# Batch 2's local score visits merged into one, a second buffer for transposed strided keys, and an undivided last sum

## The chip, the core and the metric

One core of a Trainium2 chip runs the kernel. The metric is the device time in microseconds (us) of one execution; the median of several executions stands for a kernel. A profile is one more execution, recorded by the hardware profiler.

## What is computed

Eight batches of eight-head attention over 576 positions with head size 64, then a two-layer network with squared relu:

```
scores = scale * q @ k^T                       # 8 batches, 8 heads, 576 x 576, scale 1/8
mask_local   = (rel >= 0) & (rel < 32)         # heads 0 to 3
mask_strided = (rel >= 0) & (pos % 32 equal)   # heads 4 to 7
attn = softmax(where(mask, scores, -1e9));  x = attn @ v      # -> x: 4608 x 512
out  = relu(x @ w_in) ** 2 @ w_out             # 512 -> 2048 -> 512
```

Inputs and output are fp32 in memory; the kernel computes in bf16, with fp32 sums.

## The kernel before

The network is cut into nine chunks of 512 tokens. `mm1` (L855) makes one of 16 hidden blocks: four matmuls of 128x512 into a PSUM bank (of two, "ph", in turn), a relu on ScalarE (L869), and a square on VectorE (L873), issued one step later. `mm2` (L958) is a quarter of one output block: four matmuls, after the fourth quarter a copy on ScalarE (L973) and a store through SP. The last two chunks use sums of weights and activations in seven products (`mm2_7`, L922).

The attention is woven into these groups. The main loop (L1175) counts groups n; before group n it runs the words of line n of `PLAN`. Chunk 0's mm1 are groups 0 to 15, its mm2 16 to 31, chunk 1's mm1 32 to 47, its mm2 48 to 63; chunk 2 begins at group 64, and reads tokens of batch 2. A function passed to `later(n, ...)` (L483) is issued at the end of the n-th group from there (with n = 1, the current one); `put_off` (L664) does that and also marks PSUM banks as unread, so that nobody takes them. Nothing reorders afterwards: each engine executes in the order of issue, and semaphores hold an instruction until its inputs and its buffer are ready.

Two heads make a unit; units 8 and 9 are batch 2's local heads, 10 and 11 its strided ones; 12 and 13 are batch 3's local ones. The words that matter here:

- `l`, `c`, `T`: load q or k of local units, cast to bf16 (`cast_qk_local`, L313, VectorE), and transpose on TensorE (`step_T`, L502) with a copy out of PSUM (L509). `T9kv`: unit 9's keys, copied by VectorE. `A12q`: the transpose of unit 12's queries by a DMA from SP (L403).
- `S8!` (`step_S`, L527): scores of unit 8, twelve matmuls of 128x96 (L554), alternately of the two heads in the two halves of TensorE's rows, into four PSUM banks. With "!", the four exponentials of 128x288 (L570) are issued at once, and the masks (L576, VectorE) one and two groups later. `S9!` is the same for unit 9.
- `G3` (`step_G`, L590): the scores of both local units of a batch in one visit of 24 matmuls (L599) into six banks, six exponentials of 128x384 (L610) at once, four mask products (L606). Row 0 and row 1 are the first and second heads of both units. Batches 3 to 7 use it; batch 2 uses S8 and S9. The exponentials lie in `es01`: 576 columns of unit 8, directly behind them 576 of unit 9, for each row.
- `D8.0`, `D8.1` (`step_D`, L814): exp times values for one head, six matmuls (L822), then a reciprocal (L827) and a product (L828) on VectorE. Each matmul reads 128 columns of the exponentials, from column 96 n on.
- `E8` (L837): the result is transposed into `xt` by a DMA from SP; mm1 reads `xt`.
- `H2v` (L460): a copy of batch 2's values on VectorE.
- `C4k`, `X4k` (L365, L370): load of a batch's strided q or k, and its transpose by a DMA from SP into a buffer of `strTs` (two for q, one for k). `s2` and `x2` (L679, L707): batch 2's strided scores, and its sums and output; `x2+2+5` puts the second and third part off by 2 and 5 groups. `k21v` (L386) copies a part of the strided keys.
- `Q`, `R`, `U`, `V`, `B`: other loads and copies of the following batches.

The last product of the last chunk ("3", L945) writes the right half of the last 128 rows in two sums of 128 columns (L948), each stored directly, the first by ScalarE's queue and the second by SP's (L949).

Of the kernel before, what the change touches and what calls it, by code (L numbers as in the profile page):

```python
# [10 lines left out]
AF = mybir.ActivationFunctionType  # L11
ALU = mybir.AluOpType
# [37 lines left out]
33: T8kv  # L50
34: C3q T8qv
35: T9qa
36: H2v
38: C3k S8!
39: c12kv A12k T9kv
40: c13kv A13k
41: D8.0
42: S9! D8.1
44: E8 c12qv A12q
45: k21v D9.0 c13qv A13q  # L60
46: D9.1
47: U3
48: s2 Q16k E9
50: Q17q Q16q
52: Q17k
54: x2+2+5
55: X3k X3q
56: C4k C4q
57: V3 R12kv
58: V4 R12qa  # L70
# [79 lines left out]
def kernel(  # L150
# [48 lines left out]
    v_st = rows.enter_context(tc.tile_pool(name="v_st", bufs=1, side="right"))  # L199

    PS = bass.MemoryType.PSUM
    strTs = {nm: rows.enter_context(tc.tile_pool(name=f"strT{nm}", bufs=n, side="right")) for nm, n in (("q", 2), ("k", 1))}
    psum = ctx.enter_context(tc.tile_pool(name="psum", bufs=1, space=PS))
    psb = psum.tile([128, 8, 512], FP32, name="psb")
    all_banks = [psb[:, i] for i in range(8)]
# [277 lines left out]
    def later(n, fn, key=None):  # L483
        pending.append((clock[0] + n, key, fn))
# [102 lines left out]
        later(3, lambda: expo(1, 1), u)  # L587
        later(4, lambda: masks(1), u)

    def step_G(b):  # L590

        us = (4 * b, 4 * b + 1)
        bk = [bank("pt") for _ in range(6)]
        bk = [bk[0::2], bk[1::2]]
        for t in range(2 * NL):
            for row in range(2):
                s, j = st[us[t // NL]], t % NL
                rows, c = slice(64 * row, 64 * row + 64), QL * (t % 4)
                nc.tensor.matmul(bk[row][t // 4][:, c:c + QL], s["kT"][rows, QL * j:QL * j + 128],  # L599
                                 s["qT"][rows, QL * j:QL * (j + 1)], start=True, stop=True)  # L600
        e = es01.rearrange("p (r c) -> p r c", r=2)

        def masks(row):
            x = e[:, row, 0:2 * S].rearrange("p (u t c) -> p u t c", u=2, c=QL)
            for i in range(2):
                nc.vector.tensor_tensor(x[:, i], x[:, i], mask_all, op=ALU.mult)  # L606

        for row in range(2):
            for i in range(3):
                nc.scalar.activation(e[:, row, 4 * QL * i:4 * QL * (i + 1)], bk[row][i][:, 0:4 * QL], AF.Exp, scale=scale)  # L610
            later(row + 2, lambda row=row: masks(row), ("G", b, row))

    def blocks(part):
        return range(NJ * part, min(NJ * (part + 1), NB))
# [199 lines left out]
    def step_D(u, part):  # L814
        run_due(lambda x: x[1] in (u, ("G", u // 4, part)))
        s = st[u]
        e = es01[:, 2 * ER * part + S * (u % 4):] if u > 11 else es[u % 4][:, ER * part:]
        rhs = s["v"].rearrange("p h t d -> p (h t) d")
        po = bank("pt")[:, 0:NL * (D + 1)].rearrange("p (n d) -> p n d", d=D + 1)
        for n in range(NL):  # L820
            c = QL * n
            nc.tensor.matmul(po[:, n, :], e[:, c:c + 128], rhs[:, NL * part + n, 0:D + 1], start=True, stop=True)  # L822
        if part == 0:
            s["x"] = xl_pool.tile([QL, 2 * NL, D], BF16, name="x_l")
        x = s["x"].rearrange("p (t h) d -> p h t d", h=2)[:, part]
        rinv = small.tile([128, NL, 1], FP32, name="rinv")
        nc.vector.reciprocal(rinv[0:QL], po[0:QL, :, D:D + 1])  # L827
        nc.vector.tensor_tensor(x, po[0:QL, :, 0:D], rinv[0:QL].to_broadcast([QL, NL, D]), op=ALU.mult)  # L828
# [93 lines left out]
    def mm2_7(c, i):  # L922
        n, u = ORDER7[i // 2], i % 2
        g, r0 = gs[c], 512 * c + 256 * u
        t0 = slice(256 * u, 256 * u + 128)
        if n == "1":
            ys[c, u] = [y_pool.tile([128, 512], FP32, name="y") for _ in range(2)]
            ys[c, u, "p"] = [bank("pt")]
        if n == "6":
            ys[c, u, "p"].append(bank("pt"))  # L930
        y1, y2 = ys[c, u]
        lo, hi = slice(0, 256), slice(256, 512)
        pa = ys[c, u, "p"][n not in "124"][:, lo]
        for k in range(8):
            a = g[:, k, t0] if n == "1" else g[:, 8 + k, t0] if n == "2" else \
                ss[{"6": "2", "7": "3", "4": "a", "5": "1", "3": "4"}[n]][:, k, u]
            b = w_out_b[:, k, lo] if n == "1" else w_out_b[:, 8 + k, lo] if n == "2" else \
                ts[{"6": "2", "7": "3", "4": "4", "5": "1", "3": "b"}[n]][:, k]
            nc.tensor.matmul(pa, a, b, start=k == 0 and n not in "273", stop=k == 7, skip_group_check=True)  # L939
        if n in "12":  # L940
            nc.scalar.copy((y2 if n == "1" else y1)[:, lo], pa)
            return
        to, by = {"6": (y1[:, hi], y2[:, lo]), "7": (y2[:, hi], y2[:, lo]), "4": (y2[:, lo], y2[:, hi]),
                  "5": (y2[:, hi], y2[:, hi]), "3": (y1[:, hi], y1[:, hi])}[n]
        if n == "3" and c == NCH - 1 and u:  # L945
            nc.sync.dma_start(out=out[r0:r0 + 128, lo], in_=y1[:, lo])
            for h, eng in ((0, nc.scalar), (128, nc.sync)):
                nc.vector.tensor_tensor(to[:, h:h + 128], pa[:, h:h + 128], by[:, h:h + 128], op=ALU.add)  # L948
                eng.dma_start(out=out[r0:r0 + 128, 256 + h:384 + h], in_=to[:, h:h + 128])  # L949
            return  # L950
        nc.vector.tensor_tensor(to, pa, by, op=ALU.add)  # L951
        if n in "53":
            r0 += 128 * (n == "5")
            nc.sync.dma_start(out=out[r0:r0 + 128, :], in_=y2 if n == "5" else y1)
# [40 lines left out]
    def run_step(word):  # L995
# [3 lines left out]
        if op == "w":  # L999
            warm(int(arg))  # L1000
        elif op == "c":
            cast_qk_local(int(arg[:-2]), arg[-2], ENG[arg[-1]])
        elif op == "T":
            step_T(int(arg[:-2]), arg[-2], ENG[arg[-1]])
        elif op == "W":
            step_TS(int(arg[0]), arg[1], int(arg[2]), ENG[arg[3]])
        elif op == "S":
            u, _, half = arg.rstrip("!").partition(".")
            step_S(int(u), int("!" in arg), [int(half)] if half else range(2))
        elif op == "G":  # L1010
            step_G(int(arg))
        elif op == "b":
            step_B(*(int(x) for x in arg.split(".")))
        elif op == "N":
            step_N(int(arg))
        elif op == "O":
            step_O(int(arg))
        elif op in "sx" and "." in arg:
            (step_SS if op == "s" else step_XX)(*(int(x) for x in arg.split(".")))
        elif op == "s":  # L1020
            step_S4(int(arg))
        elif op == "x":
            b, _, pace = arg.partition("+")
            step_X4(int(b), [0] + [int(x) for x in pace.split("+")])
        elif op == "k":
            step_K(int(arg[0]), int(arg[1]), ENG[arg[2]])
        elif op == "m":
            memset_later(arg[:-1], nc.gpsimd if arg[-1] == "g" else nc.vector)
        elif op == "D":
            if "." in arg:  # L1030
                u, part = arg.split(".")
                step_D(int(u), int(part))
            else:
                step_D0(int(arg))
        elif op == "E":
            step_E(int(arg.rstrip("av")), ENG.get(arg[-1]))
        elif op == "P":
            first_part(int(arg[0]), int(arg[1]))
        elif op == "H":
            shift_v_local(int(arg[:-1]), ENG[arg[-1]])  # L1040
        elif op == "C":
            load_str_tall(int(arg[:-1]), arg[-1])
        elif op == "Q":
            load_qk_rows(int(arg[:-1]), arg[-1])
        elif op == "X":
            transpose_str(int(arg[:-1]), arg[-1])
        elif op == "A":
            transpose_cast(int(arg[:-1]), arg[-1])
        elif op == "R":
            order_local(int(arg[:-2]), arg[-2], ENG[arg[-1]])  # L1050
        elif op == "Y":
            transpose_local(int(arg))
        elif op == "V":
            load_v_local_sw(int(arg))
        elif op == "U":
            load_v_str(int(arg))
        elif op == "B":
            spread_v_str(int(arg[0]), int(arg[1]), ENG[arg[2]])
        elif op == "l":
            load_qk_local_sw(int(arg[0]), [int(x) for x in arg[2:].split("+")], arg[1])  # L1060
        elif op == "r":
            load_str_rows(int(arg[0]), arg[1])
        elif op == "i":
            load_w_in(int(arg))
        elif op == "o":
            load_w_out(int(arg))
        elif op == "z":
            late_constants()
        else:
            raise ValueError(word)  # L1070
# [145 lines left out]
```

## Time and profile before

| | us |
|---|---|
| median of 3 runs | 296.67 (295.76 to 296.91) |
| profiled execution, its time | 296.19 |
| its span in the trace | 294.5 |
| TensorE busy | 285.5 |
| VectorE busy | 206.3 |
| ScalarE busy | 169.4 |
| GpSimd busy | 85.5 |

In the profile, PE is TensorE (PEld its weight loads), DVE VectorE, ACT ScalarE, POOL GpSimd, SP SyncE; a "q" behind a name is the engine's queue. L12 is line 12 of the kernel. A row of a timeline has a start, a length, engine, line, operation, output<-input, a count, and in brackets the idle time of the engine before it and what ended it. The chain of work that ended last is followed back from the last instruction, at each step to what released it. The span leaves out 1.7 us of the execution's time, which lie before and after it.

### The profile page before, as it was taken

How to read it: one execution, taken by the hardware profiler on the slowest of the kernel's cores; microseconds unless marked ns; L12 is line 12 of the kernel's file. 1: busy time of each engine (PE TensorE's matmuls, PEld its weight loads, DVE VectorE, ACT ScalarE, POOL GpSimd, SP SyncE). 2: the span in 40 equal slices, each digit the busy share in tenths (PEclk: the TensorE clock that was granted, in tenths of full speed). 3: DMA queues.
4: the chain of work that ended last, by engine and by line, in shares of the span. 5: the costliest groups of instructions: out<-in, count | busy, mean ns of one | idle time of the engine just before them, and what ended most of it. 6: DMA issues, size and time to landing. Idle time of an engine off the chain costs nothing.

```text
span 294.5 us, 6425 instructions
## 1 busy us (share of the span) xinstructions
PE 285.5 (97%) x2441; PEld 153.6 (52%) x2477; DVE 206.3 (70%) x531; ACT 169.4 (58%) x320; POOL 85.5 (29%) x133
## 2 busy tenths in 40 slices
PE   7899999999999999999999999999999999999994
PEld 3554555544445454454445444454444444984594
DVE  5667797685577755667367836683389979958983
ACT  3767846774758736674567446654675566206610
POOL 8884443073025036146400940000000014103300
PEclk9999999999999999999999999999999999999999
DMA  7999999999999999989997997521011210030003
GB/s 144 187 210 208 198 202 183 212 212 101 135 249 140 153 168 173 184 107 138 216 158 132 136 217 138 108 58 73 36 20 48 82 38 1 0 115 30 1 2 142
DMA packets 91086, 37.23 MB, mean 126 GB/s; under 512 B 77392, under 2 KB 83896, under 8 KB 91056
## 3 DMA queue, kind: packets, MB, share of 16 engines
q0 software_dynamic: 49968, 18.14, 58.9%
q1 hardware_dynamic: 40944, 18.62, 31.6%
q8 instruction: 19, 0.31, 0.4%
q14 instruction: 11, 0.09, 0.1%
q10 hardware_dynamic: 144, 0.07, 0.1%
HBM read 36.83 MB, written 9.44 MB: 157 GB/s over the span
## 4 chain that ended last, share of the span: by engine, by line
PE 93%; DMA 3%; issue 1%; POOL 1%; DVE 0%; DVEq 0%; POOLq 0%
PE psb L863 42%; PE psb L969 33%; PE psb L939 9%; DMA vl<-in_v_dram 3%; PE psb L822 2%; PE psb L599 1%; PE psb L502 1%; PE psb L554 1%; PE psb L751 1%; PE psb L687 1%; PE psb L756 1%; POOL xt L306 0%; PE psb L637 0%; PE psb L844 0%; PE psb L623 0%
## 5 line engine op out<-in xcount | busy, mean ns | idle before, releaser
L863 PE MATMUL psb<-xt,w_in 128*128 128x512 bf16 x557 | 130.8, 379 | 0.9
L869 ACT ACTIVATE r<-psb 128x512 bf16<-128x512 f32 x144 | 85.6, 599 | 46.2 <-PE psb L863 43.0
L969 PE MATMUL psb<-w_out_b,g_sb 128*128 128x512 bf16 x432 | 99.2, 379 | 1.4 <-issue 0.8
L863 PEld LDWEIGHTS <-w_in 128*128 128x128 bf16 x576 | 53.7, 98 | 60.0 <-issue 1.1
L873 DVE TENSOR_TENSOR g_sb<-r 128x512 bf16<-128x512 bf16 x112 | 46.8, 422 | 39.9 <-ACT r L869 38.7
L969 PEld LDWEIGHTS <-g_sb 128*128 128x128 bf16 x448 | 41.8, 98 | 47.5
L973 ACT COPY y<-psb 128x512 f32<-128x512 f32 x28 | 16.6, 591 | 38.9 <-PE psb L969 38.8
L908 POOL CAST sa<-g_sb 128x256 fp32r<-128x256 bf16 x16 | 9.6, 603 | 96.6 <-DVE g_sb L903 96.6
L735 DVE TENSOR_TENSOR xt<-psb,rv 64x144 bf16<-64x144 f32 x60 | 18.7, 311 | 9.2 <-ACT rv L723 8.4
L828 DVE TENSOR_TENSOR x_l<-psb,rinv 96x384 bf16<-96x384 f32 x28 | 15.5, 553 | 1.0
L606 DVE TENSOR_TENSOR e<-e,mask_all 128x576 bf16<-128x576 bf16 x20 | 8.4, 458 | 10.5 <-ACT e L610 10.3
L903 DVE TENSOR_TENSOR g_sb<-r 128x512 bf16<-128x512 bf16 x32 | 13.0, 420 | 2.9 <-ACT r L869 2.9
L610 ACT ACTIVATE e<-psb 128x384 bf16<-128x384 f32 x30 | 12.0, 513 | 4.2 <-PE psb L599 4.2
L365 POOL DMA_DIRECT2D q_t<-in_q_dram x6 | 3.2, 536 | 38.1 <-DMA qT_s<-q_t 22.4
L294 POOL DMA_DIRECT2D k_l<-in_k_dram x16 | 11.7, 736 | 4.1 <-DMA k_t<-in_k_dram 1.6
L294 POOL DMA_DIRECT2D q_l<-in_q_dram x16 | 11.6, 732 | 3.4 <-DMA k_t<-in_k_dram 2.0
L939 PE MATMUL psb<-t,s 128*128 128x256 f32 x96 | 12.2, 283 | 0.0
L365 POOL DMA_DIRECT2D k_t<-in_k_dram x6 | 3.3, 553 | 30.2 <-DMA kT_s<-k_t 28.2
L939 PEld LDWEIGHTS psb<-t,s 128*128 128x128 f32 x96 | 11.6, 188 | 0.0
L951 DVE TENSOR_TENSOR y<-psb,y 128x256 f32<-128x256 f32 x19 | 8.1, 424 | 4.3 <-PE psb L939 3.5
L453 POOL DMA_DIRECT2D vl<-in_v_dram x8 | 9.8, 1227 | 3.7 <-PE psb L969 2.8
L650 DVE TENSOR_TENSOR xt<-psb,rv 64x144 bf16<-64x144 f32 x24 | 7.5, 311 | 4.5 <-ACT rv L642 4.2
(153 smaller groups left out, 321.8 us busy)
## 6 DMA issues: line engine op xcount, KB each, us to landing
out_dram<-y SPq DMA_DIRECT2D x35, 256.0 KB, 2.8
vl<-in_v_dram POOLq DMA_DIRECT2D x8, 288.0 KB, 9.1
w_out_b<-in_moe_w_out_dram POOLq DMA_DIRECT2D x4, 512.0 KB, 14.9
q_t<-in_q_dram POOLq DMA_DIRECT2D x7, 288.0 KB, 6.6
k_t<-in_k_dram POOLq DMA_DIRECT2D x7, 288.0 KB, 6.3
w_in<-in_moe_w_in_dram POOLq DMA_DIRECT2D x2, 768.0 KB, 13.5
k_l<-in_k_dram POOLq DMA_DIRECT2D x16, 72.0 KB, 8.1
q_l<-in_q_dram POOLq DMA_DIRECT2D x16, 72.0 KB, 7.2
```

Of the source, the lines that this page charges most:

```text
L294: nc.gpsimd.dma_start(out=t[:, :, hh, :], in_=src[b, 2 * p + hh].rearrange("(t p) d -> p t d", p=QL))
L453: nc.gpsimd.dma_start(out=t[32:128, :, :, :, 0:D].rearrange("p u h t d -> p (u h t) d"), in_=v[b, 0:4].rearrange("h (t p) d -> p (h t) d", ...
L610: nc.scalar.activation(e[:, row, 4 * QL * i:4 * QL * (i + 1)], bk[row][i][:, 0:4 * QL], AF.Exp, scale=scale)
L735: nc.vector.tensor_tensor(to[:, :, :, n * part:n * (part + 1), par], both[half(par), :, 0:w].rearrange("c f (a h m) -> c h m f a", a=n, h= ...
L828: nc.vector.tensor_tensor(x, po[0:QL, :, 0:D], rinv[0:QL].to_broadcast([QL, NL, D]), op=ALU.mult)
L863: nc.tensor.matmul(ph, w_in_tile(kk, ff), xt[kk][:, 512 * c:512 * (c + 1)], start=(kk == order[0]), stop=(kk == order[-1]))
L869: nc.scalar.activation(r, ph, AF.Relu)
L873: later(1, lambda: nc.vector.tensor_tensor(g[:, ff, :], r, r, op=ALU.mult))
L903: nc.vector.tensor_tensor(g[:, ff, :], r, r, op=ALU.mult)
L939: nc.tensor.matmul(pa, a, b, start=k == 0 and n not in "273", stop=k == 7, skip_group_check=True)
L969: nc.tensor.matmul(py, g[:, ff, 128 * j:128 * (j + 1)], w_out_b[:, ff, :], start=(ff == 0), stop=(ff == 15))
L973: nc.scalar.copy(y, py)
```

## The change

Batch 2 gets one visit `G2` before group 38 in place of `S8!` (38) and `S9!` (42). `step_G` takes a list of paces, one for each of its six exponentials: the n-th is issued with its pace as the delay in groups, and its PSUM bank stays marked as unread until then. Row 0's masks follow one group behind row 0's third exponential, row 1's one group behind the sixth. `step_D` reads the layout of `es01` that G writes from unit 8 on. Unit 9's key transposes, the D and E steps, `s2` and `x2` move to other groups. `strTs` gets a second buffer for k. The last sum is one of 256 columns, and the two stores follow it.

```diff
@@ PLAN
-36: H2v
-38: C3k S8!
-39: c12kv A12k T9kv
+36: H2v T9kv
+38: C3k G2+0+1+2+4+5+6
+39: c12kv A12k
 40: c13kv A13k
-41: D8.0
-42: S9! D8.1
-44: E8 c12qv A12q
-45: k21v D9.0 c13qv A13q
-46: D9.1
-47: U3
-48: s2 Q16k E9
+43: D8.0
+44: c12qv A12q D9.0
+45: k21v c13qv A13q
+46: D8.1
+47: U3 D9.1 E8
+48: Q16k E9
+49: s2
 50: Q17q Q16q
 52: Q17k
-54: x2+2+5
-55: X3k X3q
+55: X3k X3q x2+2+4
@@ strTs
-... for nm, n in (("q", 2), ("k", 1))}
+... for nm, n in (("q", 2), ("k", 2))}
@@ step_G
-    def step_G(b):
+    def step_G(b, pace):
...
+        def expo(row, i):
+            nc.scalar.activation(e[:, row, 4 * QL * i:4 * QL * (i + 1)], bk[row][i][:, 0:4 * QL], AF.Exp, scale=scale)
+
         for row in range(2):
             for i in range(3):
-                nc.scalar.activation(e[:, row, 4 * QL * i:4 * QL * (i + 1)], bk[row][i][:, 0:4 * QL], AF.Exp, scale=scale)
-            later(row + 2, lambda row=row: masks(row), ("G", b, row))
+                put_off(pace[3 * row + i], [bk[row][i]], ("G", b, row, i), lambda row=row, i=i: expo(row, i))
+            later(pace[3 * row + 2] + (1 if pace[5] else row + 2), lambda row=row: masks(row), ("G", b, row))
@@ step_D
-        e = es01[:, 2 * ER * part + S * (u % 4):] if u > 11 else es[u % 4][:, ER * part:]
+        e = es01[:, 2 * ER * part + S * (u % 4):] if u > 7 else es[u % 4][:, ER * part:]
@@ mm2_7, the last product
+            nc.vector.tensor_tensor(to, pa, by, op=ALU.add)
             for h, eng in ((0, nc.scalar), (128, nc.sync)):
-                nc.vector.tensor_tensor(to[:, h:h + 128], pa[:, h:h + 128], by[:, h:h + 128], op=ALU.add)
                 eng.dma_start(out=out[r0:r0 + 128, 256 + h:384 + h], in_=to[:, h:h + 128])
@@ run_step
-            step_G(int(arg))
+            b, _, pace = arg.partition("+")
+            step_G(int(b), [int(x) for x in pace.split("+")] if pace else [0] * 6)
```

`put_off`, which the change calls and leaves as it is, is among the functions above or reads: mark each bank in `unread` under the key; when due, remove the marks and run the function; with a delay of 0, at once.

More of the change, by code (lines that the diff above doesn't have):

```diff
@@ L201 @@
     PS = bass.MemoryType.PSUM
-    strTs = {nm: rows.enter_context(tc.tile_pool(name=f"strT{nm}", bufs=n, side="right")) for nm, n in (("q", 2), ("k", 1))}
+    strTs = {nm: rows.enter_context(tc.tile_pool(name=f"strT{nm}", bufs=n, side="right")) for nm, n in (("q", 2), ("k", 2))}
     psum = ctx.enter_context(tc.tile_pool(name="psum", bufs=1, space=PS))
```

## The prediction

> **What bounds the kernel now.** I read the page first: busy times, then the chain of work that ended last.
>
> ```profile
> span 294.5 us, 6425 instructions
> PE 285.5 (97%) x2441; PEld 153.6 (52%) x2477; DVE 206.3 (70%) x531; ACT 169.4 (58%) x320; POOL 85.5 (29%) x133
> PE 93%; DMA 3%; issue 1%; POOL 1%; DVE 0%; DVEq 0%; POOLq 0%
> ```
>
> TensorE is busy for 97% of the span and is 93% of the chain, with 1% "issue". Only what makes TensorE do less, or stand still for less time, can change the end, apart from the last additions and stores. Next come the waits of TensorE alone:
>
> ```profile
> PE psb L969 <- issue: 0.8, 5, 0.2
> PE psb L554 <- DVE kTl L509: 0.4, 1, 0.4
> ...
> PE psb L347 <- DMA w_out_b<-in_k_dram: 0.2, 1, 0.2
> ```
>
> The only wait for a transfer is 0.2 us, in the first stage (L347). Since a matmul's end is modelled, short losses hide in "busy". They come out of the chain of work in order of time (start, length, line), where a stretch of groups can be compared with its count of matmuls. This is the stage that the change rewrites:
>
> ```profile
> 55.01 2.59 PE psb L863 x12
> 57.60 0.36 PE psb L554 x12
> 57.96 0.97 PE psb L863 x4
> 58.93 0.26 PE psb L502 x6
> ...
> 61.01 0.18 PE psb L822 x6
> 61.19 0.86 PE psb L863 x4
> 62.05 0.36 PE psb L554 x12
> 62.41 0.29 PE psb L822 x6
> 62.70 1.73 PE psb L863 x8
> ...
> 65.46 0.18 PE psb L822 x6
> ...
> 68.42 0.37 PE psb L687 x32
> ```
>
> L863 is mm1: twelve matmuls in 2.59 us, so a group of four costs 0.863. The two score visits (L554) are S8 at 57.60 and S9 at 62.05, 0.36 us each. What follows a visit costs 0.11 more than it does elsewhere: 0.97 against 0.86, and 0.29 against 0.18. Two stretches run late. From 59.19 (58.93 + 0.26) to 61.01 stand two groups, 1.73 of work in 1.82: 0.09 lost. From 62.70 to 65.46 stand three, 2.59 in 2.76: 0.17 lost. ScalarE's timeline shows why:
>
> ```profile
> 58.13 1.31 ACT L570 ACTIVATE e<-psb 128x288 bf16<-128x288 f32 x4
> 59.29 0.65 ACT L869 ACTIVATE r<-psb 128x512 bf16<-128x512 f32 x1
> ...
> 62.09 0.60 ACT L869 ACTIVATE r<-psb 128x512 bf16<-128x512 f32 x1 [0.45 <-PE psb L863]
> 62.58 1.31 ACT L570 ACTIVATE e<-psb 128x288 bf16<-128x288 f32 x4
> 63.74 1.32 ACT L869 ACTIVATE r<-psb 128x512 bf16<-128x512 f32 x2
> ```
>
> After each visit four exponentials stand in a row (1.31 us) ahead of the next relu, which frees one of mm1's two banks. The relu of the group that ended at 62.41 + 0.29 + 0.86 = 63.56 starts at 63.74 instead of directly.
>
> **The change part by part.** I set the sum against the profiled execution: 296.19 us, of which 294.5 is span. It lies 0.48 under the median of the three runs (296.67) and inside their spread (295.76 to 296.91).
>
> *One visit of 24 instead of two of 12.* Batches 3 and later already do this; the chain shows theirs:
>
> ```profile
> 83.63 2.16 PE psb L863 x10
> ...
> 98.47 0.62 PE psb L599 x24
> ```
>
> One visit costs 0.62 where two cost 0.72: -0.10. One of the two extra 0.11 behind a visit goes: -0.11. Together -0.21 us. The transposes of unit 9's keys (T9kv, 0.26) move from group 39 to 36, so they only change places.
>
> *The exponentials spread over groups 38, 38, 39, 41, 42, 43 (paces 0, 1, 2, 4, 5, 6; a pace of n is issued behind group 38 + n - 1).* Six of 128x384 replace eight of 128x288, one at a time between relus. Their step is read from batch 3:
>
> ```profile
> 99.00 2.40 ACT L610 ACTIVATE e<-psb 128x384 bf16<-128x384 f32 x6
> ```
>
> A relu takes 0.49 from its start to the next (62.09 to 62.58) and such an exponential some 0.38 (2.40 less one length of 0.51, over five), 0.87 against 0.863 per group. No relu is late by more than a tenth, and the second bank covers that. The two losses go: -0.26 us; at worst they stay, 0.
>
> *The new order of masks and D steps.* Row 0's masks are issued behind group 40, D8.0 before 43, D9.0 before 44, row 1's masks behind 44, D8.1 before 46. On VectorE, row 1's two masks thus stand behind the square of 42, D8.0's reciprocal and product, the square of 43, the cast of unit 12's queries (group 44) and D9.0's reciprocal and product. In the kernel before the same kinds of instructions stand in a row:
>
> ```profile
> 61.94 0.35 DVE L313 COPY k_l<-xt 96x768 bf16<-96x768 bf16 x1
> 62.21 0.42 DVE L873 TENSOR_TENSOR g_sb<-r 128x512 bf16<-128x512 bf16 x1
> 62.54 0.19 DVE L827 RECIPROCAL rinv<-psb 96x6 f32<-96x6 f32 x1
> 62.77 0.55 DVE L828 TENSOR_TENSOR x_l<-psb,rinv 96x384 bf16<-96x384 f32 x1
> 63.24 0.41 DVE L873 TENSOR_TENSOR g_sb<-r 128x512 bf16<-128x512 bf16 x1
> ...
> 64.26 0.44 DVE L576 TENSOR_TENSOR e<-e,mask_all 128x576 bf16<-128x576 bf16 x1
> 64.63 0.41 DVE L873 TENSOR_TENSOR g_sb<-r 128x512 bf16<-128x512 bf16 x1
> ```
>
> From one start to the next: cast 0.27, square 0.33, reciprocal 0.23, product 0.47, mask 0.37. Now both engines on one clock. TensorE: group 37 ended at 57.60; add T9k 0.26, the visit 0.62 and 0.11, and group 42 ends 5 x 0.863 later, at 62.91. Add D8.0 (0.18), 43, D9.0 (0.18), 44 and 45: D8.1 could start at 65.86. ScalarE: relu 41 starts at 62.08, the exponential behind it at 62.57, relu 42 at 62.95, and it ends at 63.55. VectorE: the square of 42 starts at 63.58; then 0.33 + 0.23 + 0.47 + 0.33 + 0.27 + 0.23 + 0.47 = 2.33, so the first mask starts at 65.91 and the second at 66.28, ending at 66.73. D8.1's sixth matmul reads 128 columns from column 480 of unit 8's half row, and the last 32 belong to unit 9: in this layout it needs the second mask too. It ends at some 66.83 instead of 66.04: **+0.80 us** of TensorE standing still. That is the price of the new wait; group 46, D9.1 and all behind them on TensorE move with it. The bounds are 0 (the masks in time) and 1.20 (below). G's other waits are hidden: unit 9's keys, copied behind H2v (0.48 from some 57.0, then the copy's 0.75), are there at about 58.1, when the visit's first twelve matmuls end; uncovered, this costs a tenth at most.
>
> A page speaks to this step: the Trainium skill, "VectorE: DVE Perf Modes", section "The DRAIN you can't avoid", says that the next instruction does not start until the pipe is empty. By it the lengths would add up, not the steps. The rows above disagree (0.42 long, the next one 0.33 later), so I take the steps.
>
> *s2 one group later, E8 and E9 later, x2 one group later.* s2 and x2 have the same lengths as before. What they hand on must be there when chunk 2 starts, at group 64:
>
> ```profile
> 65.62 2.77 SPq L837 DMA_TRANSPOSE xt<-x_l  x1
> 68.49 4.22 SPq L403 DMA_TRANSPOSE qT<-q_l  x2
> 72.81 2.07 SPq L837 DMA_TRANSPOSE xt<-x_l  x1
> ```
>
> E8 goes behind the two transposes of queries (A12q, A13q) in SP's queue; 65.62 + 4.22 + 2.77 and two short steps put E9 at about 72.8, where it was. PE needs both at 83.63 + 0.3. I cost it at 0; the rival below prices it.
>
> *Second buffer for the strided keys.* It lets the keys' transposes of batches 5 to 7 start without waiting until s4 to s6 have read the old tile, and what stands behind them in SP's queue with them. But no TensorE wait above names these tiles: 0. Bounds 0 and 0, since an earlier transfer delays nobody that TensorE waits for.
>
> *The last sum in one piece.*
>
> ```profile
> 289.60 0.42 DVE L951 TENSOR_TENSOR y<-psb,y 128x256 f32<-128x256 f32 x1 [0.52 <-PE psb L939]
> ...
> 290.54 0.49 DVE L948 TENSOR_TENSOR y<-psb,y 128x128 f32<-128x128 f32 x2 [0.52 <-PE psb L939]
> 290.87 0.37 ACTq L949 DMA_DIRECT2D out_dram<-y  x1
> 291.06 0.34 SPq L949 DMA_DIRECT2D out_dram<-y  x1
> ```
>
> Two halves end at 291.03 and their stores leave at 290.87 and 291.06. One sum of 0.42 ends at 290.96, and both leave at about 291.00: the later one 0.06 earlier, the other 0.13 later. I take -0.06; if the ScalarE queue's store sets the end, it is +0.13. The Trainium skill, "Perfetto Trace Analysis", section "Optimizing Scalar/DVE Operations", speaks against this edit ("breaking up instructions may allow work to be completed sooner"). By it the +0.13 would hold.
>
> **Sum:** -0.21 - 0.26 + 0.80 + 0 + 0 - 0.06 = +0.27 us, so 296.46 in the profiled execution's terms and 296.94 on the median. I forecast the middle, **296.7 us**: no change that can be told. (Half a per cent, 1.5 us, is about what a measurement of this kernel can tell from no change.)
>
> **The rivals.**
> - *No new wait* (the masks are in time): the other terms alone, -0.53, give 295.66 on the profiled execution and 296.14 on the median. For it: VectorE's row is full only by my sum of steps, and 0.8 us of slack would undo it. Against: every step is measured in this same stage. Chance 0.2.
> - *The end on the slow side: E9's landing becomes the bound at group 64.* The rows of L837 in this stage:
>
> ```profile
> DMA to landing us min/median/max: 9.6/10.2/10.8
> ```
>
> E9 at 72.81 lands at up to 83.6; chunk 2's second matmul needs it at about 83.63 + 0.27 + 0.22 = 84.1. It decides as soon as E9 is issued after 73.3. If the late D9.1 or E8's own 2.77 shifts it to 74.5, it lands at 85.3 and TensorE stands 1.2 us: 296.7 + 1.2 = 297.9. For it: the slack is half a microsecond, and E8 and E9 now go back to back. Against: the queue does the same work in another order and is not empty in between. Chance 0.1.
> - *VectorE one after another*, the rule above as a mechanism: 0.42 + 0.19 + 0.55 + 0.41 + 0.35 + 0.19 + 0.55 + 0.44 + 0.45 = 3.55 from 63.58, against my 3.15, makes the wait 1.20: 297.1. Chance 0.05.
> - *The split was better*: the last term +0.13 in place of -0.06: 296.9. Chance 0.05.
>
> **How the numbers follow.** The forecast has 0.55, the rivals 0.4, and 0.05 is left for what I do not see. The range reaches from the case without the wait (295.66, on the profiled execution) to the late landing (297.9), with little beyond: 295.5 to 297.9. Faster by over 0.5% needs more than all gains of this stage together: 0.05. Slower takes the late landing, in part, and half of the unseen: 0.1. Within: 0.85.
>
> **What would show it.** In the changed kernel's chain: one L598 piece of 24 at about 57.9, then groups of 0.86 without loss until D8.0; a TensorE gap of about 0.8 us at D8.1 near 66, with VectorE's second row of masks ending just before it; ScalarE's exponentials single between relus; chunk 2 starting at about 83.9 instead of 83.63; the last two stores leaving together. If D8.1 follows group 45 directly, the wait was wrong and the kernel is faster by about half a microsecond. If the first groups of chunk 2 wait on a transposed output, the second rival has it.

## The result, and the profile after

| | before | changed |
|---|---|---|
| median, us | 296.36 (22 runs) | 297.12 (22 runs) |
| profiled execution, its time | 296.19 | 297.05 |
| its span | 294.5 | 295.3 |
| groups 35 to 47 in the trace | 13.41 | 14.05 |

The ratio of the changed kernel to the one before is 1.0025 (95% interval 1.0016 to 1.0035): slower by a quarter of a per cent, 0.4 us above the forecast of 296.7, within the range and on the side of the sum's sign. The change is small, but the interval lies above 1, so it can be told, which the forecast had denied. Two of the 22 runs of the kernel before took over 303 us, and the ratio leaves them out.

The page of the changed kernel (busy time, share of the span, instructions; then the chain by engine):

```profile
span 295.3 us, 6455 instructions
PE 288.4 (98%) x2477; PEld 153.3 (52%) x2477; DVE 205.5 (70%) x530; ACT 169.5 (57%) x318; POOL 85.7 (29%) x133
PE 86%; DMA 6%; POOL 3%; DVE 2%; issue 1%; ACT 1%; POOLq 0%
```

Busy shares of the whole span hardly move, but the chain has 2% of VectorE and 1% of ScalarE where it had none. (Its larger shares of DMA and GpSimd lie ahead of this stage: before 29.2 us it follows one load of 18.01 us, where the kernel before's followed one of 7.89.) The chain in order of time shows the place (lines of the changed kernel are two or three further on: mm1 is L865, the visit L598, D's matmuls L824):

```profile
55.30 0.86 PE psb L865 x4
...
58.15 0.78 PE psb L598 x24
58.93 0.98 PE psb L865 x4
...
66.37 0.46 DVE e L605
...
66.87 0.33 PE psb L824 x5
...
67.24 0.20 PE psb L824
67.44 0.86 PE psb L865 x4
...
69.35 0.86 PE psb L971 x4
```

Group 35 starts at 55.30 (55.01 before), and 47 ends at 69.35. The visit takes 0.78, not 0.62. Group 38 ends at 59.91; four groups, D8.0, 43, D9.0, 44 and 45 would bring TensorE to 66.31 without loss (59.91 + 7 x 0.863 + 2 x 0.18). D8.1 would then end at 66.49; it ends at 67.44. That is 0.95 us of standing still, and the chain leaves TensorE there for the mask on VectorE. The waits of TensorE name it too, though the row counts only what the modelled ends leave visible:

```profile
PE psb L824 <- DVE e L605: 0.6, 1, 0.6
```

VectorE's timeline of the changed kernel, first the values' shift and the key copy, then the row ahead of row 1's masks:

```profile
57.29 0.48 DVE L459 COPY vl<-vl 32x1280 bf16<-32x1280 bf16 x1
57.70 0.74 DVE L508 COPY kTl<-psb 128x576 bf16<-128x576 bf16 x1
...
64.03 0.43 DVE L875 TENSOR_TENSOR g_sb<-r 128x512 bf16<-128x512 bf16 x1 [0.45 <-ACT r L871]
64.37 0.18 DVE L829 RECIPROCAL rinv<-psb 96x6 f32<-96x6 f32 x1
64.59 0.55 DVE L830 TENSOR_TENSOR x_l<-psb,rinv 96x384 bf16<-96x384 f32 x1
65.06 0.43 DVE L875 TENSOR_TENSOR g_sb<-r 128x512 bf16<-128x512 bf16 x1
65.41 0.35 DVE L312 COPY q_l<-xt 96x768 bf16<-96x768 bf16 x1
65.68 0.18 DVE L829 RECIPROCAL rinv<-psb 96x6 f32<-96x6 f32 x1
65.89 0.55 DVE L830 TENSOR_TENSOR x_l<-psb,rinv 96x384 bf16<-96x384 f32 x1
66.37 0.81 DVE L605 TENSOR_TENSOR e<-e,mask_all 128x576 bf16<-128x576 bf16 x2
```

From the square of 42 (64.03) to the end of the second mask (67.18) it is 3.15 us without a pause, the very sum of steps in the prediction.

Two parts of an execution frame this stage, and the experiments need both. Up to group 35 the executions scatter: it started between 54.55 and 55.81 in the eleven profiles of this study, whatever the kernel. From the end of group 47 to the last matmul it is 222.10 us before, 222.03 in the changed kernel, and between 222.01 and 222.04 in e3 to e7 and e9 (290.52 and 291.38 are the ends of the last matmul). It is longer in e1 (222.37), e2 (222.45) and e8 (227.04). So what differs is read from groups 35 to 47, in which a single execution shows hundredths. Of e1 to e4 there is only the one profiled execution each, so that their times say nothing; from e5 on there are 12 or 13 runs each.

### The profile page after: what moved, and what is told of

Read it like the earlier page. It is cut to its first block, busy times and chain, and to the rows that moved or that the text cites. A ratio compares the mean times of both kernels' runs of the same rounds, so it can differ in the third digit from the quotient of the medians.

```text
span 295.3 us, 6455 instructions
## 1 busy us (share of the span) xinstructions
PE 288.4 (98%) x2477; PEld 153.3 (52%) x2477; DVE 205.5 (70%) x530; ACT 169.5 (57%) x318; POOL 85.7 (29%) x133
## 4 chain that ended last, share of the span: by engine, by line
PE 86%; DMA 6%; POOL 3%; DVE 2%; issue 1%; ACT 1%; POOLq 0%
PE psb L865 37%; PE psb L971 33%; PE psb L941 9%; DMA xt<-in_k_dram 6%; PE psb L824 2%; PE psb L598 1%; POOL w_in L464 1%; POOL xt L305 1%; PE psb L753 1%; PE psb L501 1%; PE psb L689 1%; PE psb L758 1%; DVE g_sb L875 0%; PE psb L639 0%; POOL vl L452 0%
## 5 line engine op out<-in xcount | busy, mean ns | idle before, releaser
L865 PE MATMUL psb<-xt,w_in 128*128 128x512 bf16 x576 | 132.1, 379 | 0.0
L971 PE MATMUL psb<-w_out_b,g_sb 128*128 128x512 bf16 x448 | 101.4, 379 | 0.0
L865 PEld LDWEIGHTS <-w_in 128*128 128x128 bf16 x576 | 53.6, 98 | 59.9 <-issue 0.6
L737 DVE TENSOR_TENSOR xt<-psb,rv 64x144 bf16<-64x144 f32 x60 | 18.7, 312 | 6.2 <-ACT rv L725 5.3
L605 DVE TENSOR_TENSOR e<-e,mask_all 128x576 bf16<-128x576 bf16 x24 | 10.0, 456 | 11.0 <-ACT e L608 10.8
L608 ACT ACTIVATE e<-psb 128x384 bf16<-128x384 f32 x36 | 15.0, 509 | 4.2 <-PE psb L598 4.2
L824 PEld LDWEIGHTS <-e 128*128 128x128 bf16 x168 | 8.0, 97 | 5.7 <-DVE e L605 1.2
```

What stands on the lines that cost most here:

```text
L737: nc.vector.tensor_tensor(to[:, :, :, n * part:n * (part + 1), par], both[half(par), :, 0:w].rearrange("c f (a h m) -> c h m f a", a=n, h= ...
L865: nc.tensor.matmul(ph, w_in_tile(kk, ff), xt[kk][:, 512 * c:512 * (c + 1)], start=(kk == order[0]), stop=(kk == order[-1]))
L971: nc.tensor.matmul(py, g[:, ff, 128 * j:128 * (j + 1)], w_out_b[:, ff, :], start=(ff == 0), stop=(ff == 15))
```

## The experiments

My theory: TensorE stands because row 1's masks come late in VectorE's order (0.95) and the key copy stands behind the values' shift (0.16); without these two waits the change wins half a microsecond. The rivals: the masks are late because of the put-off exponentials on ScalarE; VectorE is so full that the wait only moves; the second buffer is to blame.

**e1: D8.1 one group later.**

```diff
-46: D8.1
-47: U3 D9.1 E8
+47: U3 D8.1 D9.1 E8
```

> The changed kernel, with D8.1 moved from group 46 to group 47, ahead of D9.1. Theory (TensorE stands at D8.1 because row 1's masks come late on VectorE, at the end of a row of work that is independent of where D8.1 stands): one group of 0.86 us now runs in the wait, so of the 0.95 us that TensorE lost at D8.1 (the first piece of D8.1 in the chain follows group 45's end by that much) about 0.1 is left, and s2 starts 0.85 earlier, counted from group 35's start: 13.2 instead of 14.05 (less group 48's 0.86). Rival (the loss is work that the new order makes unavoidable on TensorE or ScalarE, wherever D8.1 stands): the gap moves to group 47 and s2 starts at the same distance. The key copy's wait inside the visit (0.78 instead of 0.62) stays in both.

Its chain (L823 are D's matmuls), and the cast on VectorE:

```profile
66.91 0.20 PE psb L823 x5
...
67.16 0.39 PE psb L823 x7
...
68.41 0.86 PE psb L970 x4
```

```profile
65.15 0.54 DVE L311 COPY q_l<-xt 96x768 bf16<-96x768 bf16 x1
```

Groups 35 to 47 take 13.37 us (55.04 to 68.41): 0.68 less than in the changed kernel, where I expected 0.85. D8.1 and D9.1 take 0.64 instead of 0.36, so 0.28 of the wait is left; the cast was 0.19 longer in this execution, and so the masks came later. The group run inside the wait hides most of it: the loss hangs on where D8.1 stands against the masks. Some 0.3 us were lost again in chunk 2 of this execution, where the chain leaves TensorE for copies on VectorE (the 222.37 above).

**e2: the cast out of VectorE's row.**

```diff
-44: c12qv A12q D9.0
-45: k21v c13qv A13q
-46: D8.1
+44: D9.0
+45: k21v c13qv A13q
+46: D8.1 c12qv A12q
```

> The changed kernel, with the cast of unit 12's queries (0.27 us on VectorE from its start to the next) moved from group 44 to behind D8.1 at 46; exponentials, masks and D steps stay. Theory (VectorE's row sets the end of row 1's masks, its steps add up): the masks end 0.27 us earlier and TensorE's gap at D8.1 falls from 0.95 to about 0.68. Rival A (row 1's last exponential, put off by six groups on ScalarE, sets the masks): the gap stays at 0.95. Rival B (VectorE works strictly one after another, so whole lengths count): the gap falls by the cast's length, 0.35.

```profile
57.46 0.78 PE psb L598 x24
58.24 0.32 PE psb L865
...
65.91 0.33 PE psb L824 x5
...
66.48 0.22 PE psb L865
```

The visit ends at 58.24; with 0.11 behind it, eight groups and two D steps, D8.1 would start at 65.62 and end at 65.80. It ends at 66.48: 0.68 of wait, as the sum of steps says. The wait shrank by the cast's step, 0.27, though the exponentials kept their places. That rules out ScalarE, and the length of 0.35. The move had a price elsewhere: A12q now starts later on SP's queue, E8 and E9 behind it. TensorE's waits and the landing of L839's two transposes, which were issued at 71.53 and 74.10:

```profile
PE psb L865 <- DMA xt<-x_l: 0.3, 1, 0.3
```

```profile
DMA to landing us min/median/max: 9.9/10.4/10.8
```

This is the prediction's second rival, in small: issued 1.3 us after 72.81, E9 held chunk 2's second matmul for 0.3 us.

**e3: the six exponentials at once.**

```diff
-38: C3k G2+0+1+2+4+5+6
+38: C3k G2
```

> The changed kernel, with the six exponentials of G2 issued at once (no paces, row 0's masks behind group 39, row 1's behind 40). Theory (four exponentials in a row cost TensorE 0.09 and 0.17 us before, since relu stands behind them; the paces took that away and brought the late masks): the gap at D8.1 is gone (-0.95), but group 38's relu now starts behind six exponentials (2.4 us after the visit), about 1.15 us late, and group 40 waits for its bank: about 1.0 us lost there. In sum within 0.2 us of the changed kernel. Rival (the paces were not needed, since two banks absorb a burst): no loss at group 40, and s2 0.9 us earlier than in the changed kernel.

ScalarE's timeline, and TensorE's waits:

```profile
58.65 2.40 ACT L608 ACTIVATE e<-psb 128x384 bf16<-128x384 f32 x6
60.87 1.16 ACT L871 ACTIVATE r<-psb 128x512 bf16<-128x512 f32 x2
```

```profile
PE psb L865 <- ACT r L871: 0.9, 1, 0.9
```

The wait at D8.1 is gone (D8.1 takes 0.18), and group 40 waits for its bank, behind a relu that starts at 60.87. The row counts 0.9 us; by the stage it is 1.0, since groups 35 to 47 take 14.12 and would take 13.10 without either wait (14.05 - 0.95). So the paces are worth as much as the late masks cost: the burst of six costs 1.0, the paced six nothing by themselves.

**e4: the key copy ahead of the values' shift.**

```diff
-36: H2v T9kv
+36: T9kv H2v
```

> The changed kernel, with T9kv issued ahead of H2v at group 36, so that VectorE copies unit 9's keys before it shifts the values. Theory (the visit's second half waits for that copy, which ended at 58.44 in a visit from 58.15): the copy ends 0.4 us earlier, the visit takes 0.62 instead of 0.78 us, and all behind it moves by -0.16; the gap at D8.1 stays 0.95, since VectorE's row behind it hangs on group 42's relu. Rival (a visit of 24 matmuls of two units is slower because of its two key tiles, not because of the copy): 0.78 stays.

```profile
57.45 0.62 PE psb L598 x24
...
66.54 0.20 PE psb L824
66.74 0.22 PE psb L865
```

```profile
64.54 0.52 DVE L312 COPY q_l<-xt 96x768 bf16<-96x768 bf16 x1
```

The visit takes 0.62: the 0.16 were the copy. D8.1 ends 1.13 late instead of 0.95, since the cast again took longer (0.52, 0.17 more), so the stage is 14.06 long, where 13.89 was expected.

**e5: masks ahead of the row.** Row 1's masks are issued one group earlier, with e4's edit.

```diff
-36: H2v T9kv
-38: C3k G2+0+1+2+4+5+6
+36: T9kv H2v
+38: C3k G2+0+1+2+3+4+5
```

> The changed kernel, with paces 0, 1, 2, 3, 4, 5 in place of 0, 1, 2, 4, 5, 6 (so row 1's masks are issued behind group 43 instead of 44, ahead of the square of 43, the cast and D9.0's product on VectorE) and T9kv ahead of H2v. Theory (the 0.95 us at D8.1 come from where row 1's masks stand in VectorE's order, the 0.16 inside the visit from where the key copy stands): both go, what is left is the gain, and groups 35 to 47 take 14.05 - 0.95 - 0.16 = 12.94 us in the trace, against 13.41 in the kernel before; ratio to the kernel before about 0.998 (-0.5 us). Rival A (VectorE is full in this stage, so the work that the masks pass is late in turn and TensorE stands elsewhere, at a bank or at D8.1 and D9.1): 13.6 to 14.0 us. Rival B (without the empty place between the third and the fourth exponential the relus fall behind): up to 0.3 us lost at groups 42 to 44.

```profile
57.70 0.62 PE psb L598 x24
58.32 4.42 PE psb L865 x20
62.74 0.18 PE psb L824 x6
...
65.70 0.18 PE psb L824 x6
65.88 0.87 PE psb L865 x4
...
67.80 0.86 PE psb L971 x4
```

Five groups behind the visit take 4.42, which is 5 x 0.863 and the 0.11, and each D step 0.18. Groups 35 to 47 take 12.95 us (54.85 to 67.80); 12.94 was expected. Both waits are gone and none has come in their place. From there to the last matmul it is no longer than before (222.03 against 222.10), so nothing is given back later in this execution. The median was 295.64 us (12 runs) against 296.12; the ratio is 0.9990 (0.9969 to 1.0010), so the trace shows the 0.46 us and the times do not settle it.

**e6: the second buffer alone**, in the kernel before.

```diff
-... (("q", 2), ("k", 1))}
+... (("q", 2), ("k", 2))}
```

> The kernel before with the second buffer for transposed strided keys, and nothing else of the change. Theory (no TensorE wait hangs on those tiles): the keys' transposes of batches 5 to 7 start up to 3 us earlier on SP's queue, TensorE's stages keep their lengths, ratio 1.000 within 0.001. Rival (the buffer moves the other tiles in memory, or the earlier transposes collide with other transfers, and part of the loss of the changed kernel is from there): ratio up to 1.0025.

SP's timeline, batch 6's keys, and the chain's first and last pieces around the stage:

```profile
150.30 1.37 SPq L370 DMA_TRANSPOSE kT_s<-k_t  x1
```

```profile
55.81 2.59 PE psb L863 x12
...
69.22 0.37 PE psb L687 x32
```

The transpose starts earlier (152.68 in the kernel before), and TensorE's stage keeps its 13.41 us. The ratio is 0.9998 (0.9981 to 1.0015). By the trace the buffer is worth nothing and costs nothing; the times leave half a microsecond open to either side.

**e7: e1 and e4 together.**

```diff
-36: H2v T9kv
+36: T9kv H2v
-46: D8.1
-47: U3 D9.1 E8
+47: U3 D8.1 D9.1 E8
```

> The changed kernel, with D8.1 at group 47 ahead of D9.1 and T9kv ahead of H2v; paces and masks stay. Theory: the gap at D8.1 falls from 0.95 to between 0.1 and 0.3 (it had 0.28 left in the run with D8.1 alone moved, where the cast on VectorE took 0.54 instead of 0.35), the visit takes 0.62; groups 35 to 47 take 13.1 to 13.3 us, against 13.41 in the kernel before; ratio 0.9985 to 0.9995. Rival (the masks' place costs the same wherever D8.1 stands): 13.9 us, ratio 1.002.

```profile
66.25 0.45 PE psb L823 x12
66.71 0.86 PE psb L864 x4
```

The two D steps take 0.45 instead of 0.36, and groups 35 to 47 13.02 us, less than the 13.1 to 13.3 expected, because the cast took 0.35 this time. Ratio 0.9994 (0.9977 to 1.0011).

**e8 and e9: e5's kernel and the changed kernel once more, side by side.**

> The kernel of e5 (paces 0 to 5, T9kv ahead of H2v) once more, beside the changed kernel on the same chip, because its interval (0.9969 to 1.0010) left open whether it beats the kernel before. Theory: groups 35 to 47 take 12.95 us again, and the ratio is 0.998 with an upper end below 1. Rival (the 0.46 us won in the stage are given back later): the stage is as short, but the distance from s2 to the last matmul grows, and the ratio is 1.000.

> The changed kernel itself once more, beside e8. Theory: groups 35 to 47 take 14.05 us as in its first profile, ratio 1.002 to 1.0025, and e8 is 1.1 us (0.4%) faster than it. Rival (the 14.05 were one execution's): another length of the stage, nearer to 13.4.

e8: groups 35 to 47 take 12.94 us (54.92 to 67.86). The ratio is 0.9989 (0.9964 to 1.0015), a second point on the same side and again not settled; its upper end stayed above 1, and the medians are level (296.02 and 296.03). So that e5's kernel beats the kernel before is shown by its stage and not by its times. The execution of e8 that was profiled happened to take 300.62 us, and its trace shows where most of the excess came from, in TensorE's timeline at chunk 2 and later, and in L839's landings:

```profile
84.50 0.39 PE L865 MATMUL psb<-xt,w_in 128*128 128x512 bf16 x1 [1.19 <-DMA xt<-x_l]
86.25 5.99 PE L865 MATMUL psb<-xt,w_in 128*128 128x512 bf16 x27 [1.35 <-DMA xt<-x_l]
...
119.76 2.53 PE L865 MATMUL psb<-xt,w_in 128*128 128x512 bf16 x11 [1.83 <-DMA xt<-x_l]
```

```profile
DMA to landing us min/median/max: 10.7/11.1/11.5
```

E8 and E9 were issued at 73.00 and 75.49 there, since the two queries' transposes ahead of them took 6.91 us of SP's queue. TensorE stood 1.19 and 1.35 us for them, and 1.83 us for a later transposed output: 4.4 of the 5.0 us that the way from group 47 to the last matmul was longer. It is the second rival at more than its full size, in one execution, and no difference between kernels is read from it. A shorter stage brings chunk 2 nearer to these landings: in e5 E9 was issued at 72.9 and landed after 10.0 us, 0.3 us before chunk 2's second matmul (83.01 + 0.22). Whether this is why the times do not show the stage's gain is not shown.

e9: 14.31 us (54.80 to 69.11), 0.26 more than the first profile, with the cast at its longest:

```profile
64.91 0.61 DVE L312 COPY q_l<-xt 96x768 bf16<-96x768 bf16 x1
```

Ratio 1.0016 (0.9992 to 1.0041), so this repetition alone does not settle that the changed kernel is slower; its stage is again longer than the 13.41 of the kernel before. Side by side on one chip its median was 0.76 us above e8's (296.78 and 296.02), where 1.1 was expected.

## Why the prediction was right

- **The new wait (+0.80): right in mechanism and place, 0.15 too small.** VectorE's row was 3.15 us long, as summed, and TensorE arrived when it was expected to, counted from group 35's start with the 0.16 of the visit. What I mis-sized is the handing over: I gave D8.1 0.10 us behind the second mask's end, and it took 0.26 (67.18 to 67.44): the sixth matmul starts at 67.24 and takes 0.20. e2 shows that VectorE's order sets the wait, by an edit of one known size; e5 shows that it goes when the masks are issued ahead of the row.
- **The visit (-0.21): right, but 0.16 of it was taken back.** e4 and e5 show 0.62 with 0.11 behind it. In the changed kernel the second half waits for the key copy. I had put this at "a tenth at most", with the copy there at 58.1, 0.24 behind the visit's start; it ended 0.29 behind it (58.44), and its price was 0.16.
- **The spread exponentials (-0.26): right.** Behind the visit, groups 38 to 42 take their 5 x 0.863 in the changed kernel and in e5, and e3 shows that a burst does cost TensorE a bank.
- **Second buffer (0): right** by e6's trace; no other run has it by itself.
- **The last sum (-0.06): not found.** The changed kernel's rows:

```profile
291.40 0.42 DVE L949 TENSOR_TENSOR y<-psb,y 128x256 f32<-128x256 f32 x1 [0.52 <-PE psb L941]
291.85 0.40 SPq L951 DMA_DIRECT2D out_dram<-y  x1
291.86 0.37 ACTq L951 DMA_DIRECT2D out_dram<-y  x1
```

The stores leave 0.47 us behind the last matmul (291.38) where the later one left 0.54 behind it before (291.06 less 290.52), as foreseen. But the end did not come sooner. The packed traces give the spans to a nanosecond (294.482 before, 295.334 in the changed kernel); from the last matmul to the span's end it is 3.96 and 3.94 us with two pieces (before, e6) and between 3.95 and 3.98 with one (the changed kernel and the other experiments). Neither the -0.06 nor the +0.13 of the fourth rival is there: the end did not follow the departure of either store. What else sets it, no run shows, and the edit was not tried by itself.
- **The sum.** In the stage: -0.26 - 0.21 + 0.16 + 0.95 = +0.64, and 14.05 - 13.41 is 0.64. The forecast had +0.33 there, half of it: the handing over (0.15) and the key copy (0.16) were both set too low. The medians differ by 0.76, and the interval of the ratio is 0.5 to 1.0 us. The range of the forecast, 2.4 us, held a gain as well as a loss, so that the time fell inside it says little; what bears the mechanism out is the stage.
- **The rivals.** VectorE one after another is ruled out by the 3.15 and by e2. The late landing was absent in the changed kernel's profile, where E8 and E9 were issued from 69.62 on and landed after 7.7 and 9.5 us, but it showed in e2 and in one execution of e8. The kernel before lives close to it too: 72.81 + 9.6 to 10.8 against 83.85. How often it strikes, I have not measured.
- **A gap in its reading.** The prediction's list of TensorE's waits begins behind the longest one, 1.3 us at L986, ahead of the execution's first matmul. It is 1.3 us in all eleven profiles, so nothing here hangs on it.

## What to carry to other kernels

When work is merged and put off to relieve one engine, write down the order that results on the next engine, and add up the steps from one start to the next: here VectorE's nine instructions gave the wait to within the handing over. Put an instruction on which the bounding engine waits ahead of those that nobody waits for yet; moving the masks by one group was worth 0.95 us of TensorE's time in the trace. And where single executions scatter in a part that the change does not touch, compare the stage that it does touch.

## What the runs showed that I had not expected

The cast of unit 12's queries (by its row, a copy from bf16 to bf16) took 0.35 us in the kernels before and after and in e2, e3, e6, e7 and e8, but 0.54, 0.52, 0.55 and 0.61 in e1, e4, e5 and e9. In these four GpSimd was issuing loads at that time, yet so it was in the changed kernel's first profile, in e7 and in e8, where the cast took 0.35. The Trainium skill, "SBUF — State Buffer", section "Who interferes with whom", says that a copy on VectorE can run in a mode with two ports, in which it and GpSimd shut each other out of a shared pair of ports. The four agree with it and the three do not show it, so the cause stays open. The longer cast makes a wait such as the one at D8.1 longer in some executions (14.31 against 14.05 us).
